# Column sums of an output weight: VectorE additions in a tail, or accumulating DMA transfers during the attention

## The chip, the cores and the metric

One core of one Trainium2 chip runs the whole program in one launch. The metric is device time in microseconds (us) from start to end of the program, the median of several runs. Engines are named as the profile names them: PE (TensorE matmul), PEld (its weight load), DVE (VectorE), ACT (ScalarE), POOL (GpSimd) and SP (SyncE, which here only issues DMA transfers).

## What is computed

An attention over 4 batches, 8 heads, 576 positions and 64 columns feeds two feed-forward layers in a row, on 2304 tokens with 512 columns and 2048 hidden columns. The change is in layer 1, whose constant `b` is applied in a cheaper place than the reference writes it:

```python
def _moe_ref(x, w_in, w_out, s, b):
    h = x @ w_in
    r = np.maximum(h, 0.0)
    g = s * (r * r) + b
    return (g @ w_out).astype(np.float32)
```

Since `b` is one number, `b @ w_out` is `b` times the column sums of `w_out`: 512 numbers, the same for every token. The kernel leaves `b` out of layer 1, computes these sums once, and adds them to the tokens when layer 2 loads them.

## The kernel before

Fp32 products run as products of two rounded pieces, a high and a low one (`woh` and `wol` for layer 1's output weight, `wih` and `wil` for its input weight). Each weight piece lies in SBUF in four buffers (r = 0 to 3) of 128 partitions x 4 x 512 numbers, 1 MB each. They are made in the first 175 us by `convert` and then stay until layer 1 is over.

The stages overlap. The attention runs unit by unit (a batch and a head, `unit`). Each unit loads `qk`, `qn` and `vx` through SP; POOL makes the first 64 columns of the weights `Pt` (line 557) from `ex` (line 500) and scales two of the five tiles (line 571); PE transposes the tiles (line 598) and multiplies them with `V` (line 626). Between the attention's products PE does layer 1 for the tokens already there (lines 832 and 901, blocks of 256 tokens), and when the attention is over, two blocks of 512 tokens: this is **layer 1's tail**. In the tail the weights of layer 2 are converted as well (`convert`, lines 690 to 707, by ACT, DVE and POOL), combined (`combine_in` and `combine_out`, line 743), split (`split`, lines 728 and 729) and stored in DRAM. Layer 2 follows (lines 1034 and 1100).

No engine's order is written by hand. Every piece of work is a step with an engine, an estimated duration, a priority (a lower number goes first), an extra `lag` until its result is there, and the steps that it must follow. `Plan.order` plays this through and gives each engine one fixed order; on the chip each engine then works down its own list, waiting at each instruction for what it needs. So an instruction whose input comes later than planned holds up everything behind it on its engine. POOL and SP also issue DMA transfers in this order.

The column sums are `column_sums`, with priority 700, behind most else. After `begin`, a step in the first block of the tail, DVE adds the 16 + 16 slices of `woh` and `wol` into `total` (lines 800 and 802, 31 additions of 128 x 512). One PE product with a matrix of ones (line 822) sums over the 128 partitions, into a bank of the ring `h`, whose two banks also take layer 1's first products; ACT reads those banks at line 877. `pick` (lines 815 and 817) moves the 512 sums into `bcs`, one number per partition and column group. Layer 2's loads add `bcs` at line 959.

Of the kernel before, what the change touches and what calls it, by code (L numbers as in the profile page):

```python
# [9 lines left out]
F32 = mybir.dt.float32  # L10
# [4 lines left out]
AF = mybir.ActivationFunctionType  # L15
ALU = mybir.AluOpType
# [3 lines left out]
P = 128  # L20
# [3 lines left out]
PE, ACT, DVE, POOL, DMA = range(5)  # L24
# [29 lines left out]
def dve_us(n, fast=False):  # L54
    return 0.068 + (0.00052 if fast else 0.00104) * n
# [123 lines left out]
class Plan:  # L179
# [29 lines left out]
    def add(self, engine, us, prio, f, r=(), w=(), after=(), keep=(), share=1.0):  # L209


        bufs = list({id(b): b for b in (*r, *w, *keep) if b.ring is not None}.values())
        new = [b for b in bufs if b.maker is None]
        waits = {id(s): s for b in r for s in b.writers}
        waits.update((id(s), s) for s in after)
        s = Step(engine, us, prio, f, list(waits.values()), bufs, new)
        s.share = share
        s.left = len(waits)
        for x in waits.values():
            x.next.append(s)  # L220
        for b in bufs:
            b.users += 1
            if b.maker is None:
                b.maker = s
            elif id(b.maker) not in waits:
                b.maker.next_start.append(s)
                s.left += 1
        for b in w:
            b.writers.append(s)
        self.steps.append(s)  # L230
        return s
# [100 lines left out]
def attention_then_two_ffn(ctx: ExitStack, tc: tile.TileContext, qk, qz, vm, beta,  # L332
# [3 lines left out]
    nc = tc.nc  # L336
# [8 lines left out]
    NR = 4  # L345
    FPR = NFC // NR
# [4 lines left out]
    NB1 = len(blocks1)  # L351
# [8 lines left out]
    plan = Plan()  # L360
    add = plan.add
# [3 lines left out]
    dram = ctx.enter_context(tc.tile_pool(name="dram", bufs=1, space=DRAM))  # L365
# [4 lines left out]
    mask = const.tile([P, SP], BF16, name="mask")  # L370
# [10 lines left out]
    WOD = dram.tile([P, 3, NQ2 // 2, DH], F32, name="wo_d")  # L381
    WIS = [dram.tile([P, 2, 2, 4, P], F32R, name=f"wi_split{q}_d") for q in range(NQ2)]
    WOS = [dram.tile([P, 7, 2, NQ2 // 2, DH], F32R, name=f"wo_split{x}_d") for x in range(2)]
    x_in = {(b, g): Buf() for b in range(B) for g in range(2)}
    y_in = {j: Buf() for j in range(NT // N1)}
    wi_in, wo_in, wi_split = ({} for _ in range(3))
# [22 lines left out]
    R = {}  # L409
# [249 lines left out]
    W = {}  # L659
# [6 lines left out]
    def w_at(nm, r, j):  # L666
        return W[nm, r].t[:, j]
# [65 lines left out]
    def load_us(n):  # L733
        return n * 512 / 310e3
# [31 lines left out]
    def combine_out(prio, q, w0, w1):  # L766
# [4 lines left out]
        def b_(i, j):  # L771
            return (w0, w1)[i].t.bitcast(F32)[:, j * DH:(j + 1) * DH]

        def t_(i):
            return sc.t[:, i - 1]

        sums(prio, [sc, w0, w1], [lambda: (t_(1), b_(0, 1), b_(0, 0), ALU.subtract), lambda: (t_(2), b_(1, 1), t_(1), ALU.subtract),
                                  lambda: (t_(3), b_(1, 1), b_(0, 1), ALU.subtract), lambda: (t_(4), b_(1, 0), t_(2), ALU.subtract)])
        d, x = WOS[q // 4], q % 4
        if q < 4:  # L780
# [11 lines left out]

    def column_sums(prio, begin):

        total, ps = Buf(R["total"], [P, 512]), Buf(R["h"], [P, 512])

        def more(r, j, nm):
            x = w_at(nm, r, j).bitcast(F32)
            if r == j == 0 and nm == "wol":
                nc.vector.tensor_tensor(total.t, w_at("woh", 0, 0).bitcast(F32), x, op=ALU.add)  # L800
            elif r + j:
                nc.vector.tensor_tensor(total.t, total.t, x, op=ALU.add)

        for r in range(NR):
            for j in range(FPR):
                def pair(r=r, j=j):
                    more(r, j, "woh")
                    more(r, j, "wol")

                add(DVE, dve_us(512) * (2 if r + j else 1), prio, pair, [W["woh", r], W["wol", r]] + [total] * (r + j > 0), [total],  # L810
                    after=[begin] * (r + j == 0))

        def pick():
            for ec in range(NCC):
                nc.vector.tensor_tensor_reduce(total.t[:, ec * P:(ec + 1) * P], ps.t[:, ec * P:(ec + 1) * P], ident, 1.0, 0.0,
                                               ALU.mult, ALU.add, bcs[:, ec:ec + 1])
            nc.vector.tensor_scalar(bcs, bcs, sb[:, 1:2], None, op0=ALU.mult)

        plan.steps[-1].lag = 12.0
        ones = Buf(R["ones"], [P, P])  # L820
        add(ACT, 0.2, prio, lambda: nc.scalar.activation(ones.t, mask[:, :P], AF.Copy, bias=1.0), after=[begin], w=[ones])
        add(PE, 0.87, prio, lambda: nc.tensor.matmul(ps.t, ones.t, total.t, start=True, stop=True), [ones, total], [ps])
        add(DVE, 1.0, prio, pick, [ps, total], [sums_in, total])

# [13 lines left out]
    def load_x(j, prio):  # L838

        t0, n = blocks1[j]  # L840
        big = n > N1
        xh, xl = xs[j] = [[Buf(R[x], [P, NCC // (1 + big), n], F32R) for _ in range(1 + big)]
                          for x in (("yh", "yl") if big else ("xh", "xl"))]
        edge = len(TA) * P - D
        need = [x_in[b, g] for b in range(B) for g in range(2)
                if b * S + g * edge < t0 + n and b * S + (edge, S)[g] > t0]
        for c in range(NCC):
            xr, half = Buf(R["yr" if big else "xr"], [P, n]), Buf()
            add(DMA, 0.002 * n, prio, lambda c=c, xr=xr: nc.sync.dma_start(xr.t, x_d[:, c, t0:t0 + n]), need, [xr])
            add(ACT, act_us(n), prio, lambda c=c, xr=xr: nc.scalar.copy(x_at(xh, c), xr.t), [xr], [xh[c * len(xh) // NCC], half])  # L850
            add(DVE, dve_us(n), prio, lambda c=c, xr=xr: nc.vector.tensor_tensor(x_at(xl, c), xr.t, x_at(xh, c).bitcast(F32),
                                                                                 op=ALU.subtract),
                [xr, half], [xl[c * len(xl) // NCC]])
# [152 lines left out]
    def load_wo(blk, p, half):  # L1006
# [7 lines left out]
        else:  # L1014
            add(POOL, 1.0, prio, lambda: nc.gpsimd.dma_start(w.t, WOS[half][:, slot]), need, [w]).lag = 3.0 + load_us(8 * DH)  # L1015
        return w
# [153 lines left out]
    opened = add(NONE, 0.0, 0.0, open_second, after=attention_steps)  # L1170
# [5 lines left out]
    def rank1(i):  # L1176
        i += max(0, i - NFC * (NB1 - NBIG))
        return UNIT0 + UNIT * (i + LEAD) / PER_UNIT
# [3 lines left out]
    for i in range(len(seq) + LAG1):  # L1182
        if i < len(seq):
            j, fc = seq[i]
            begin = len(plan.steps)
            if fc == 0:
                load_x(j, -1.0)
                accs[j] = [Buf(R[x], [P, 512]) for x in BANKS[j]]
            n = len(plan.steps)
            halves[i] = first(j, fc, rank1(i), -1.0)  # L1190
            in_steps[fc // FPR] += [x for x in plan.steps[n:] if x.engine == PE]
            if j < NB1 - NBIG:
                small_steps += plan.steps[begin:]
            if (j, fc) == (NB1 - 2, 4):
                begin_sums = plan.steps[-1]
        if i >= LAG1:
            j, fc = seq[i - LAG1]
            n = len(plan.steps)
            y_part(j, fc, accs[j], *halves.pop(i - LAG1), rank1(i) + 0.01)
            out_steps[fc // FPR] += plan.steps[n:]  # L1200
            begin = n
            if fc == NFC - 1:
                n = len(plan.steps)
                y_out(j, accs[j], -1.0)
            if j < NB1 - NBIG:
                small_steps += plan.steps[begin:]
            if fc == NFC - 1:
                if j == NB1 - NBIG - 1:
                    small_left = add(NONE, 0.0, 0.0, close_small, after=small_steps)
                if j == NB1 - 2:  # L1210
                    banks_left = add(NONE, 0.0, 0.0, lambda: None, after=[x for x in plan.steps[n:] if x.engine != DMA])
        if i == len(seq) - 1:
            left = [add(NONE, 0.0, 0.0, lambda: None, after=in_steps[r]) for r in range(NR)]
            inputs_left = add(NONE, 0.0, 0.0, lambda: None, after=[*left, *plan.steps[layer1:]])
    out_left = [add(NONE, 0.0, 0.0, lambda: None, after=out_steps[r]) for r in range(NR)]
    column_sums(700.0, begin_sums)
    closed = add(NONE, 0.0, 0.0, close_first, after=plan.steps[layer1:])
    low, high = Home(m1t, "low", 1024), Home(m1t, "high", 2560, F32R)
# [102 lines left out]
```

## Time and profile before

| | |
|---|---|
| median of 3 runs | 1045.85 us (1044.26 to 1050.34) |
| the profiled execution | 1047.84 us, span 1046.1 us |
| busy share | PE 96%, PEld 89%, DVE 83%, ACT 65%, POOL 27% |
| mean granted clock of TensorE | 0.986 |
| moved by DMA | 188.63 MB |

The span runs from the first to the last instruction of the profiled execution. A busy share is an average over stages that have different limits: a stage is read from the busy times of its own stretch and from the waits there. An idle time names its releaser, the work that ended last before the waiting instruction could go.

### The profile page before, as it was taken

To read this page: it belongs to the slowest core of one execution; us is meant where nothing else is said; L and a number is where in the kernel's file an instruction comes from. 1 tells how busy PE (TensorE), PEld (TensorE's weight loads), DVE (VectorE), ACT (ScalarE), POOL (GpSimd) and SP (SyncE) were. 2 spreads that over 40 slices of the span, in tenths; PEclk is the share of its full clock that TensorE was granted. 3 is DMA by queue.
4 is the path that set the end of the run, shared out by engine and by line. 5 is a ranking of instruction groups with operands and counts; after the bars stand their busy time and mean duration, and the time that the engine had idled before them with its cause. 6 is when DMAs were issued, how large, how long until landed. Compare 5 with 4: busy or idle time off the path is not lost. (4 is left out here: it accounts for less than half of the span.)

```text
span 1046.1 us, 20182 instructions
## 1 busy us (share of the span) xinstructions
PE 1004.7 (96%) x6710; PEld 926.6 (89%) x6710; DVE 870.4 (83%) x2399; ACT 680.0 (65%) x1575; POOL 280.6 (27%) x386
## 2 busy tenths in 40 slices
PE   6889997999999999999997999999999999999998
PEld 4657787999999999999885778899989999999998
DVE  6898999999999999975699989459985779757865
ACT  6876887888888787766644686446653456534552
POOL 6864354333334244312223330000110000100010
PEclk9998998999999999999999899999999999999999
DMA  9663563323422432307857886758686666776564
GB/s 257 181 193 107 154 205 97 109 88 99 138 87 88 122 94 88 103 24 240 244 159 217 256 286 227 272 165 290 216 307 209 222 211 203 248 250 196 178 216 167
DMA packets 88984, 188.63 MB, mean 180 GB/s; under 512 B 8752, under 2 KB 63024, under 8 KB 81584
## 3 DMA queue, kind: packets, MB, share of 16 engines
q1 hardware_dynamic: 81392, 135.95, 41.3%
q0 software_dynamic: 7056, 51.38, 14.5%
q8 instruction: 53, 0.87, 0.3%
q14 instruction: 51, 0.42, 0.1%
q10 hardware_dynamic: 432, 0.01, 0.0%
HBM read 144.32 MB, written 42.99 MB: 179 GB/s over the span
## 5 line engine op out<-in xcount | busy, mean ns | idle before, releaser
L1100 PE MATMUL bank<-woh,S 128*128 128x256 f32 x792 | 106.3, 281 | 2.6 <-DMA woh<-wo_split_d 1.8
L1100 PEld LDWEIGHTS bank<-woh,S 128*128 128x128 f32 x792 | 99.4, 189 | 3.2 <-issue 1.9
L1100 PE MATMUL bank<-wol,S 128*128 128x256 f32 x720 | 96.8, 281 | 0.0
L557 POOL TENSOR_SCALAR Pt<-ex,nm 128x64 f32<-128x64 f32 x148 | 73.9, 511 | 84.3 <-PE bank L598 45.1
L1034 PE MATMUL bank<-wi,woh 128*128 128x384 f32 x426 | 93.8, 335 | 0.6 <-DMA woh<-wi_split_d 0.6
L554 ACT ACTIVATE Pt<-Pt,mx 128x64 f32<-128x64 f32 (+4 forms) x148 | 81.8, 555 | 16.9 <-DVE mx L545 16.2
L1100 PEld LDWEIGHTS bank<-wol,S 128*128 128x128 f32 x720 | 90.5, 190 | 0.0
L707 POOL TENSOR_TENSOR stage<-stage 128x512 int32<-128x512 int32 x36 | 49.5, 1374 | 105.9 <-DVE stage L705 67.2
L1034 PEld LDWEIGHTS bank<-wi,woh 128*128 128x128 f32 x426 | 75.6, 188 | 1.3 <-DMA woh<-wi_split_d 0.8
L598 PE MATMUL bank<-ident,Pt 128*128 128x128 f32 x432 | 66.7, 281 | 10.1 <-POOL Pt L571 7.7
L1034 PE MATMUL bank<-wi,wol 128*128 128x384 f32 x294 | 75.9, 334 | 0.0
L606 DVE TENSOR_TENSOR PTl<-bank,PTh 128x128 fp32r<-128x128 f32 (+1 forms) x144 | 63.8, 480 | 2.2 <-ACT PTh L603 1.4
L598 PEld LDWEIGHTS bank<-ident,Pt 128*128 128x128 f32 x432 | 50.0, 143 | 15.5 <-POOL Pt L571 10.5
L571 POOL TENSOR_SCALAR Pt<-Pt,rs 128x64 f32<-128x64 f32 x64 | 45.5, 754 | 67.8 <-DVE rs L576 51.7
L1015 POOL DMA_DIRECT2D wol<-wo_split_d x17 | 9.2, 541 | 200.4 <-DVE wi L729 107.1
L545 DVE CUSTOM_DVE_ANT_0 Pt<-bank,mask 128x320 f32<-128x320 f32 (+3 forms) x148 | 59.2, 416 | 3.9 <-PE bank L541 2.0
L603 ACT CAST PTh<-bank 128x128 fp32r<-128x128 f32 (+1 forms) x144 | 55.1, 431 | 3.0 <-PE bank L598 1.7
L901 PE MATMUL bank<-gh,wol 128*128 128x256 f32 x320 | 54.0, 292 | 0.0
L901 PE MATMUL bank<-gl,woh 128*128 128x256 f32 x320 | 54.0, 291 | 0.0
L1034 PEld LDWEIGHTS bank<-wi,wol 128*128 128x128 f32 x294 | 53.0, 188 | 0.4
L901 PE MATMUL bank<-gh,woh 128*128 128x256 f32 x320 | 52.6, 287 | 0.0
L832 PE MATMUL bank<-xh,wi 128*128 128x256 f32 x320 | 50.6, 289 | 0.7 <-DVE rt L881 0.6
(290 smaller groups left out, 2962.0 us busy)
## 6 DMA issues: line engine op xcount, KB each, us to landing
wol<-wo_split_d POOLq DMA_DIRECT2D x17, 1024.0 KB, 5.6
woh<-wo_split_d POOLq DMA_DIRECT2D x16, 1024.0 KB, 5.6
qk<-in_qk SPq DMA_DIRECT2D x24, 608.0 KB, 3.8
stage<-in_w_out SPq DMA_DIRECT2D x23, 512.0 KB, 4.3
wo_split_d<-high SPq DMA_DIRECT2D x44, 256.0 KB, 3.4
stage<-in_w_in SPq DMA_DIRECT2D x21, 512.0 KB, 4.6
stage<-wi_d SPq DMA_DIRECT2D x24, 384.0 KB, 4.8
wi_split_d<-woh SPq DMA_DIRECT2D x8, 1024.0 KB, 4.9
```

What stands on the lines that cost most here:

```text
L545: nc.vector.tensor_tensor_reduce(Pt[t].t[:, D + lo:D + hi], ps.t[:, :hi - lo], mask[:, SP - w + lo:SP - w + hi], -SCALE, mx.t[:, t:t + 1] ...
L554: nc.scalar.activation(Pt[t].t[:, D:w + D], Pt[t].t[:, D:w + D], AF.Exp, bias=mx.t[:, t + i:t + i + 1], scale=-1.0, accum_out=rs.t[:, t:t ...
L557: add(POOL, 0.3, lambda: nc.gpsimd.tensor_scalar(Pt[t].t[:, :D], ex.t[:, t, :], nm.t[:, t:t + 1], 1.0, op0=ALU.mult, op1=ALU.mult), [ex, n ...
L571: (nc.vector if e == DVE else nc.gpsimd).tensor_scalar(x, x, r, None, op0=ALU.mult)
L598: nc.tensor.transpose(ps.t[:, c - c0, :], Pt[t].t[:, c * P:(c + 1) * P], ident)
L603: (nc.vector.tensor_copy if dve else nc.scalar.copy)(PT[0].t[:, at_], ps.t[:, :n])
L606: nc.vector.tensor_tensor(PT[1].t[:, at_], ps.t[:, :n], PT[0].t[:, at_].bitcast(F32), op=ALU.subtract)
L707: add(POOL, 1.23 if layer == 1 else 1.45, prio, lambda: nc.gpsimd.tensor_tensor(w.t, w.t, words()[:, :, 0], op=ALU.add), [raw, low_words, ...
L832: nc.tensor.matmul(ph, w_at(nm, r, cc)[:, o:o + P], x_at(x, cc), start=(part == 0 and cc == 0), stop=(part == 2 and cc == NCC - 1))
L901: nc.tensor.matmul(acc[ec // per].t[:, (ec % per) * n:(ec % per + 1) * n], w_at(nm, r, jj)[:, ec * P:(ec + 1) * P], t(x), start=(big and f ...
L1034: nc.tensor.matmul(ps.t[:, :H2], w[i // 4].t[:, j, kk, i % 4], x[kk].t[:, k], start=begin and part == kk == 0, stop=part == 2 and kk == 1, ...
L1100: nc.tensor.matmul(acc[t].t[:, :DH], s.t[:, j, t * P:(t + 1) * P], x.t[:, k, q % 4], start=q == part == 0, stop=q == NQ2 - 1 and part == 2)
```

## The change

The 31 additions on DVE go. In their place the eight 1 MB buffers `woh` and `wol` are piled up in a DRAM tensor `pile_d`, during the attention: SP copies the first, and POOL issues seven transfers that add to what lies there (`accum_op`). Each must wait until the one before it has landed, since it reads and rewrites the same bytes. Then SP copies the first quarter of the pile to `fold_d`, POOL adds the other three quarters to it with three accumulating transfers of 256 KB, and SP loads the result into `total`. The steps start after the first product of layer 1's second block (`begin` is now in block 1). The load into `total` and the matrix of ones wait for the end of the attention (`opened`), where their buffers are made. The PE product and `pick` stay as they are.

```diff
+    pile_d, fold_d = dram.tile([P, FPR, 512], F32, name="pile_d"), dram.tile([P, 512], F32, name="fold_d")
...
-        total, ps = Buf(R["total"], [P, 512]), Buf(R["h"], [P, 512])
-
-        def more(r, j, nm):
-            x = w_at(nm, r, j).bitcast(F32)
-            if r == j == 0 and nm == "wol":
-                nc.vector.tensor_tensor(total.t, w_at("woh", 0, 0).bitcast(F32), x, op=ALU.add)
-            elif r + j:
-                nc.vector.tensor_tensor(total.t, total.t, x, op=ALU.add)
...
-                add(DVE, dve_us(512) * (2 if r + j else 1), prio, pair, [W["woh", r], W["wol", r]] + [total] * (r + j > 0), [total],
-                    after=[begin] * (r + j == 0))
+        total, ps, piled, folded = Buf(R["total"], [P, 512]), Buf(R["h"], [P, 512]), Buf(), Buf()
+        pile, fold = pile_d, fold_d
+
+        def pile_up(i, x):
+            if i == 0:
+                add(DMA, 4.0, prio, lambda: nc.sync.dma_start(pile, x()), [W["woh", 0]], [piled], after=[begin]).lag = 2.0
+            else:
+                add(POOL, 1.0, prio, lambda: nc.gpsimd.dma_start(pile, x(), accum_op=ALU.add),
+                    [W["wol" if i % 2 else "woh", i // 2], piled], [piled]).lag = 20.0
+
+        for i in range(2 * NR):
+            pile_up(i, lambda i=i: W["wol" if i % 2 else "woh", i // 2].t.bitcast(F32))
+        add(DMA, 1.0, prio, lambda: nc.sync.dma_start(fold, pile[:, 0]), [piled], [folded]).lag = 4.0
+        for j in range(1, FPR):
+            add(POOL, 1.0, prio, lambda j=j: nc.gpsimd.dma_start(fold, pile[:, j], accum_op=ALU.add),
+                [piled, folded], [folded]).lag = 10.0
+        add(DMA, 1.0, prio, lambda: nc.sync.dma_start(total.t, fold), [folded], [total], after=[opened]).lag = 3.0
...
-        plan.steps[-1].lag = 12.0
         ones = Buf(R["ones"], [P, P])
-        add(ACT, 0.2, prio, lambda: nc.scalar.activation(ones.t, mask[:, :P], AF.Copy, bias=1.0), after=[begin], w=[ones])
+        add(ACT, 0.2, prio, lambda: nc.scalar.activation(ones.t, mask[:, :P], AF.Copy, bias=1.0), after=[opened], w=[ones])
...
-            if (j, fc) == (NB1 - 2, 4):
+            if (j, fc) == (1, 0):
                 begin_sums = plan.steps[-1]
```

Through the attention the lists of PE, DVE and ACT stay as they were, but for one exchange of neighbours among PE's products. (Behind the change, lines of the file are one or two higher: 557 becomes 558, 571 becomes 572.) What changes there is POOL's list, by ten transfers, and SP's, by three. POOL in the middle of the attention, before, where line 500 makes `ex` from the loaded `qn`, line 571 scales two tiles and line 557 starts the next five:

```order
L500 TENSOR_SCALAR ex_4165<-qn_4120 128x320 [waits DMAHW6_49,Pool_49]
L571 TENSOR_SCALAR Pt_1_4061<-Pt_1_4061,rs_4063 128x64 [waits DVE_49,Activation_49]
L571 TENSOR_SCALAR Pt_1_4068<-Pt_1_4068,rs_4063 128x192 [waits Activation_49]
L557 TENSOR_SCALAR Pt_0_4237<-ex_3953,nm_4092 128x64 [waits DVE_49]
L557 TENSOR_SCALAR Pt_0_4250<-ex_3953,nm_4092 128x64
```

and at the same place now:

```order
L501 TENSOR_SCALAR ex_4173<-qn_4128 128x320 [waits DMAHW7_49,Pool_49]
L572 TENSOR_SCALAR Pt_1_4069<-Pt_1_4069,rs_4071 128x64 [waits DVE_49,Activation_49]
L572 TENSOR_SCALAR Pt_1_4076<-Pt_1_4076,rs_4071 128x192 [waits Activation_49]
L803 DMA pile_d<-woh_0_1884 128x2048 [waits DMASW4_49]
L558 TENSOR_SCALAR Pt_0_4246<-ex_3961,nm_4100 128x64 [waits DVE_49]
L558 TENSOR_SCALAR Pt_0_4259<-ex_3961,nm_4100 128x64
```

The sixth accumulating transfer has come between line 571's and line 557's work, and it waits (`DMASW4`) for the fifth to have landed. DVE in the tail, before, where the additions begin:

```order
L705 SCALAR_TENSOR_TENSOR low<-raw_7239,low 128x512
L800 TENSOR_TENSOR total_7337<-woh_0_500,wol_0_524 128x512
L802 TENSOR_TENSOR total_7337<-total_7337,woh_0_500 128x512
L802 TENSOR_TENSOR total_7337<-total_7337,wol_0_524 128x512
...
L884 TENSOR_TENSOR xh_7361<-g_7317,xh_7361 128x512
L704 TENSOR_SCALAR low<-low 128x512
```

and now:

```order
L706 SCALAR_TENSOR_TENSOR low<-raw_7257,low 128x512
L884 TENSOR_TENSOR xh_7324<-g_7285,xh_7324 128x512
L744 TENSOR_TENSOR sc_7341<-stage 128x2x128
L744 TENSOR_TENSOR sc_7341<-sc_7341,stage 128x2x128
```

The additions are gone, and layer 1's own line 884 and the combining of layer 2's weights (line 743, now 744) have moved up. PE at the sums' product (line 822), before, between two groups of line 901, where the first tail block is at the third of `woh`'s four buffers:

```order
L832 MATMUL bank_107<-yl_6923,wih_0_1550 128x512 x2
L901 MATMUL bank_111<-xh_7652,woh_0_1326 128x512
...
L822 MATMUL bank_108<-total_7337,ones_7328 128x512
L901 MATMUL bank_111<-xh_7652,wol_0_1331 128x512
```

and now:

```order
L832 MATMUL bank_109<-yl_6941,wi_742 128x512 x2
L901 MATMUL bank_113<-xh_7166,woh_0_502 128x512
...
L822 MATMUL bank_110<-total_6898,ones_6859 128x512
L901 MATMUL bank_113<-xh_7166,wol_0_526 128x512
```

The product stands 180 rows of PE's list earlier, where that block is still at the first buffer. All bank numbers are two higher, because of the two new tensors.

## Rows read from the trace of the kernel before

**Rows 1.** The page: busy time of each engine, share of the span, instructions.

```profile
PE 1004.7 (96%) x6710; PEld 926.6 (89%) x6710; DVE 870.4 (83%) x2399; ACT 680.0 (65%) x1575; POOL 280.6 (27%) x386
```

**Rows 2.** Busy time by stretch: us, PE, PEld, DVE, ACT, POOL, clock, DMA share, GB/s.

```profile
200.00:475.00 275.00, 272.83 (x2209) 267.52 (x2208) 252.67 (x974) 218.53 (x603) 97.36 (x161) 1.00 0.32 95
500.00:515.00 15.00, 15.00 (x71) 12.35 (x70) 7.20 (x15) 10.39 (x19) 5.31 (x4) 1.00 0.79 237
515.00:560.00 45.00, 45.00 (x196) 36.42 (x195) 44.05 (x67) 22.70 (x39) 12.54 (x9) 1.00 0.61 185
560.00:585.00 25.00, 18.94 (x62) 13.38 (x61) 22.99 (x50) 15.40 (x32) 7.38 (x6) 0.80 0.84 264
...
600.00:610.00 10.00, 7.81 (x33) 5.67 (x32) 7.03 (x12) 8.12 (x16) 4.53 (x3) 1.00 0.86 294
```

**Rows 3.** Busy time by stretch, within the tail's stall.

```profile
575.00:580.00 5.00, 4.18 (x10) 3.06 (x10) 4.86 (x7) 2.50 (x7) 2.98 (x2) 0.50 0.87 283
```

**Rows 4.** Timeline of PE: start, us, engine, line, operation, [idle before <- releaser].

```profile
304.67 0.60 PE L598 MATMUL bank<-ident,Pt 128*128 128x128 f32 x4
...
558.47 1.10 PE L832 MATMUL bank<-yl,wih 128*128 128x512 f32 x4
559.41 1.08 PE L901 MATMUL bank<-xh,woh 128*128 128x512 f32 x4
...
571.57 2.07 PE L822 MATMUL bank<-total,ones 128*128 128x512 f32 x2 [4.62 <-ACT g L877]
...
583.89 1.10 PE L832 MATMUL bank<-yh,wi 128*128 128x512 f32 x4
```

**Rows 5.** Timeline of ACT at the stall.

```profile
568.37 0.71 ACT L728 CAST high<-low 128x256 fp32r<-128x256 f32 x2 [6.23 <-POOL low L707]
```

**Rows 6.** Timeline of POOL: attention (the places of the transfers), then the stall.

```profile
189.30 1.52 POOL L557 TENSOR_SCALAR Pt<-ex,nm 128x64 f32<-128x64 f32 x3
...
283.00 1.78 POOL L557 TENSOR_SCALAR Pt<-ex,nm 128x64 f32<-128x64 f32 x3
...
303.01 1.40 POOL L571 TENSOR_SCALAR Pt<-Pt,rs 128x64 f32<-128x64 f32 x2
...
328.58 1.01 POOL L500 TENSOR_SCALAR ex<-qn 128x320 f32<-128x320 f32 x1
...
355.64 1.01 POOL L500 TENSOR_SCALAR ex<-qn 128x320 f32<-128x320 f32 x1 [1.93 <-DMA qn<-in_qz]
...
567.00 1.33 POOL L707 TENSOR_TENSOR low<-low,raw 128x512 int32<-128x512 int32 x1 [1.15 <-DVE low L705]
```

**Rows 7.** DVE's groups from 500 to 620 us: busy, mean ns of one | idle before.

```profile
L802 DVE TENSOR_TENSOR total<-total,wol 128x512 f32<-128x512 f32 x15 | 14.4, 959 | 0.5
L802 DVE TENSOR_TENSOR total<-total,woh 128x512 f32<-128x512 f32 x15 | 13.5, 901 | 0.1
```

**Rows 8.** Timeline of DVE: the last addition, and the step that POOL awaited.

```profile
562.80 0.69 DVE L802 TENSOR_TENSOR total<-total,wol 128x512 f32<-128x512 f32 x1
...
566.18 0.69 DVE L705 SCALAR_TENSOR_TENSOR low<-raw,low 128x512 int32<-128x512 int32 x1
```

**Rows 9.** Waits of the whole span, by who waited: us, times, longest.

```profile
PE bank L901 <- DVE yr L921: 2.0, 1, 2.0
```

**Rows 10.** DMA issues: queue, count, KB each, median us from issue to landing.

```profile
wol<-wo_split_d POOLq DMA_DIRECT2D x17, 1024.0 KB, 5.6
...
wi_split_d<-woh SPq DMA_DIRECT2D x8, 1024.0 KB, 4.9
```

**Rows 11.** Transfers of `wo_split_d`: min/median/max ns of POOL's issue, and landing.

```profile
L1015 POOL DMA_DIRECT2D wol<-wo_split_d x17: 527/527/757, 737.6 to 1021.7; - x17
...
DMA to landing us min/median/max: 2.1/4.9/9.7
```

**Rows 12.** Loads of `qn`, 185 to 345 us: us from issue to landing.

```profile
DMA to landing us min/median/max: 2.2/2.3/3.3
```

**Rows 13.** SP's timeline: the issue behind the copy into `fold_d`.

```profile
353.13 0.33 SPq L480 DMA_DIRECT2D qn<-in_qz  x1
```

More of the change, by code (lines that the diff above doesn't have):

```diff
@@ L793, in column_sums @@
     def column_sums(prio, begin):
-        total, ps = Buf(R["total"], [P, 512]), Buf(R["h"], [P, 512])
-        def more(r, j, nm):
-            x = w_at(nm, r, j).bitcast(F32)
-            if r == j == 0 and nm == "wol":
-                nc.vector.tensor_tensor(total.t, w_at("woh", 0, 0).bitcast(F32), x, op=ALU.add)
-            elif r + j:
-                nc.vector.tensor_tensor(total.t, total.t, x, op=ALU.add)
[L804 to L808, printed above, removed]
-                add(DVE, dve_us(512) * (2 if r + j else 1), prio, pair, [W["woh", r], W["wol", r]] + [total] * (r + j > 0), [total],
-                    after=[begin] * (r + j == 0))
+        total, ps, piled, folded = Buf(R["total"], [P, 512]), Buf(R["h"], [P, 512]), Buf(), Buf()
[13 more added lines that the diff above has]
+        add(DMA, 1.0, prio, lambda: nc.sync.dma_start(total.t, fold), [folded], [total], after=[opened]).lag = 3.0
         def pick():
```

## The prediction

> **What bounds the kernel now.** I read the page's busy shares first: PE is busy for 96% of the span, 1004.7 us [rows 1]. So only some 41 us without PE work can be won, and any work taken from another engine counts only where PE waits for it. Next come the busy times by stretch [rows 2]. From 200 to 475 us, where the attention runs, PE is idle for 2.2 us of 275. DVE is busy for 253 of them, POOL for only 97, and the DMA engines for a third. From 515 to 560 us DVE has 44.05 us of work in 45: that is where the additions lie. Right behind, from 560 to 585 us, PE is idle for 6.1 us and the granted clock drops to a mean of 0.80. The reader is to see this pair: a full DVE first, an idle PE afterwards.
>
> The timeline of PE shows what it costs [rows 4]. Unhindered, four products of line 901 or 832 start every 0.93 us (558.47 to 559.41). Between the starts at 559.41 and 583.89 us lie 14 such groups and the sums' product. At the usual pace that is 14 x 0.93 = 13.0 us, plus 1.1 us for the sums' product, whose two passes show as 2.07 us at a lowered clock; I take half. It took 24.5 us, so **10.4 us are lost**. One part is the 4.62 us of waiting in front of line 822; another is the clock, which from 575 to 580 us is 0.50, the 1.2 GHz level, after PE had stood idle [rows 3].
>
> Who is late is read backwards. Line 822 waits for ACT, which has to empty a bank at line 877 [rows 4]. ACT had stood idle for 6.23 us, until 568.37, at a rounding step ahead of that in its list, waiting for POOL's line 707 [rows 5]. POOL started that step at 567.00, after DVE's line 705 [rows 6]; DVE started it at 566.18, having worked almost without a gap since 515 [rows 2, 8]. The additions themselves ended at 563.5 [rows 8], so the sum is not what was awaited: the additions stood in the queue ahead of the conversion.
>
> **The change, part by part.** *Removed:* 31 additions on DVE. The 30 of line 802 take 14.4 + 13.5 us [rows 7], and one of line 800 about 0.7, in all 28.6 us. Undisturbed, one takes 0.69 [rows 8], so 31 x 0.69 = 21.4 us are the additions' own; the other 7.2 are stretching, which may fall on other DVE work instead. Of DVE's 67.0 us of work in the 70 us from 515 to 585 [rows 2] some 45.6 remain, 65%. A queue that was at most 10 us late, with 21 us of its work gone, has no reason to be late: I take the 10.4 us as won. Layer 2's conversions then become the next thing that could be late, and what covers them is that third of DVE's time.
>
> *A second stall:* from 600 to 610 us PE is idle for 2.2 us [rows 2], most of it behind DVE's line 921 [rows 9]. It is the tail of the same backlog or something of its own. Ends: 0 and 2.2 us won; I take half, 1.1.
>
> *Moved:* the sums' product and `pick`. On the present clock the product now falls between 500 and 515 us, and `pick`, about 1 us of DVE's time, with it, where DVE is busy for 7.2 us of 15 [rows 2]. The product now takes the bank that is not being filled at that point, so it need not wait for the group just ahead. Its matrix of ones is one short ACT step, earlier by the same distance. I cost all this at nothing; without that DVE cover it would be about 1 us. The load of `total` stands at the attention's end, about 475 us, some 30 us ahead of its use. The last transfer is issued about two units, 25 us, behind the first quarter-size one of 356.7 [rows 6], so the chain could be 80 us late before this load noticed.
>
> *Added:* three transfers on SP and ten on POOL. Issuing a plain 1 MB transfer takes POOL 0.53 us [rows 11], so ten take 5.3 us, in a stage where POOL is idle for 178 of 275 us [rows 2]: nothing, if they don't wait. SP's three issues cost 0.5 us each at most, with nothing waiting at those points.
>
> *The new waits.* Each accumulating transfer holds POOL's list until the one before it has landed, and lines 500, 557 and 571 are queued behind it. Line 571 is the tight one: POOL ends a pair at 304.4 [rows 6] and PE transposes tiles of that set from 304.67 on [rows 4], so a delay there reaches PE nearly whole. What counts is the spacing. On the present clock the first one falls at 190.8, the fifth at 284.2 (after two of three), the sixth at 304.4 and the seventh at 329.6 us [rows 6]. Six gaps make 138.8 us, 23.1 on average; the smallest, fifth to sixth, is 20.2. SP's copy into `fold_d` must be past by 353.1, where the next `qn` load is issued [rows 13]: 23.5 us after the seventh. The first quarter-size transfer stands behind line 500 at 356.7 [rows 6]. So a **landing time T under about 20 us costs nothing**; above 23.1 the delay is at least 6T - 138.8 us.
>
> No row shows an accumulating transfer. A plain 1 MB store takes 4.9 us and a plain 1 MB load 5.6 [rows 10]. This one must read source and destination and write the destination: never less than 4.9 us; one read and one write in sequence make 10.5; three moves of 1 MB in sequence, each as slow as the slowest landing of such loads, 9.7 [rows 11], make 29. I take 10.5, nearest to the rows that move 1 MB between SBUF and DRAM, and keep 4.9 and 29. Both 4.9 and 10.5 cost no wait.
>
> *Traffic:* seven times 3 MB and some small change, beside a third of busy DMA engines. The loads of `qn` land in 2.3 us [rows 12], and POOL already waits for some of them. About 15 fall into the time of the transfers; with T at 10.5 of 23.1, some seven overlap one. If these took twice as long and nothing covered it, that would be 16 us; most have line 557's or other work between them and line 571. Ends 0 and 16; I take 2.
>
> A rule of the skill speaks against this part. The rows first: POOL's 1 MB issues take 527 ns in the middle and 757 at most, beside a busy DVE [rows 11]. By the Trainium skill, "SBUF — State Buffer", section "SBUF: two separate sides", GpSimd can't write the descriptors of its transfers while VectorE runs an instruction in a mode that holds their shared port pair. By the rows the issues cost nothing more; by the rule each could be held for one DVE instruction, which would show as issues longer than 757 ns. No row here shows the attention's DVE work beside an issue.
>
> **The sum.** Against the profiled execution's own 1047.84 us: -10.4 - 1.1 + 2 = -9.5. That execution is 2.0 us above the median, 1045.85, for which the trace has no reason. I take the same 9.5 off the median: **1036.3 us**.
>
> **The rivals.** *POOL waits for its own transfers* (0.15, slower). Decides from T: at 24.7 us, 6T - 138.8 is 9.4, and the gain is used up. At the upper end of 29 it is 35 us: 1045.85 - 9.5 + 35 = 1071. For it: three moves of data, and SP's loads in between. Against it: 1 MB one way takes 5 us, so T would have to be five times that.
>
> *The transfers disturb the attention's loads* (0.15, about 1047). All of 14 us more than I took: 1036.3 + 14 = 1050 at the end, some 1045 in the middle. For it: PE, DVE and POOL's line 571 have no room in that stage. Against it: the DMA engines are two thirds free. The Trainium skill, "DMA: Bandwidth & Descriptors", section "Issuing engines are not separate DMA queues", says that transfers of all issuing engines share the same 16 DMA engines and interleave.
>
> *The stall stays* (0.10, 1041 to 1045). The change doesn't do what it says, as the tail still converts layer 2's weights through DVE, POOL and ACT in fixed order, and POOL's steps stretch DVE's. Half the 10.4 remaining gives 1041.5. For it: DVE's 65% holds stretched steps that the plan doesn't know. Against it: 21 us less in a queue that was late by 10.
>
> **How the numbers follow.** My forecast has 0.60, from 1032.0 (both stalls gone, no disturbance, and the fastest run's 1.6 us below the median: 1045.85 - 12.6 - 1.6 = 1031.7) to about 1040.5. A measurement of this kernel can tell about 0.5%, 5.2 us, from no change: below 1040.6 is faster, above 1051.1 slower. Faster: 0.60 and a little of the stall's rival, 0.62. Slower: the waiting rival and some of the disturbance, 0.17. The rest, 0.21, is the same. The range reaches over the second and third rival to 1051.0 and leaves out the waiting rival and what is below 1032.
>
> **What would show it.** Right: no wait of PE at line 822, the clock at 1.00 from 560 to 585 us less the shift, DVE busy for some 65% there; accumulating transfers that land within 20 us, and no POOL wait for a `pile_d` transfer in front of line 558 or 572. Disturbance would show as longer `qn` and `qk` landings and new PE idle time between 200 and 400 us. The prediction is wrong if T exceeds 24 us, or if ACT still waits several us for line 707 in the tail.

## The result, and the profile after

The changed kernel takes **1061.55 us** (median of 4 runs, 1061.2 to 1061.96) against 1047.03 for the kernel before, run beside it: a ratio of 1.0137, with a 95% interval of 1.0106 to 1.0169. It is 14.5 us slower, where the forecast had it 9.5 us faster, and above the predicted range. The profiled execution took 1061.39 us, with a span of 1059.6.

The tail did what was predicted. The busy times by stretch of the kernel after, with the columns of [rows 2]:

```profile
200.00:475.00 275.00, 255.49 (x1990) 248.44 (x1991) 237.34 (x925) 200.95 (x556) 99.73 (x163) 0.97 0.46 121
515.00:560.00 45.00, 45.00 (x217) 37.23 (x216) 29.98 (x66) 27.91 (x49) 16.02 (x11) 1.00 0.82 243
560.00:585.00 25.00, 25.00 (x109) 20.23 (x109) 17.50 (x33) 16.85 (x31) 8.94 (x6) 1.00 0.86 262
```

From 515 to 585 us PE has no gap and its clock stays at 1.00, where [rows 2] had 18.94 us of 25 at 0.80; DVE has 47.5 of 70 us of work, 68%. The loss is in the first row, the attention: PE is idle for 19.5 us there, and was for 2.2 [rows 2]. Its mean clock is 0.97: 3% of 275 us are another 8 us. Together that is some 25 us, and 27 with the 1.8 us in which PE is idle from 195 to 200 (below). A gain of some 12 in the tail and a loss of some 27 in the attention make the 14.5.

The same view of the kernel after, in steps of 5 us beside three of the seven transfers, which POOL issues at 191.55, 270.82 and 301.69 us:

```profile
195.00:200.00 5.00, 3.17 (x26) 2.94 (x24) 1.18 (x13) 2.27 (x9) 0.70 (x2) 1.00 1.03 234
200.00:205.00 5.00, 1.75 (x7) 1.75 (x8) 2.88 (x9) 0.85 (x2) 0.08 (x1) 0.64 0.64 193
...
275.00:280.00 5.00, 0.96 (x9) 0.76 (x7) 1.42 (x4) 0.14 (x1) 1.70 (x4) 0.99 1.00 256
280.00:285.00 5.00, 4.38 (x19) 4.33 (x20) 3.62 (x12) 3.42 (x10) 0.00 (x0) 0.50 0.38 132
...
305.00:310.00 5.00, 4.79 (x39) 4.56 (x37) 5.00 (x20) 3.63 (x11) 0.00 (x0) 1.00 0.94 198
310.00:315.00 5.00, 0.87 (x5) 0.87 (x5) 0.88 (x5) 0.84 (x2) 2.37 (x4) 0.90 0.24 73
```

First the DMA share rises to about 1 (last column but one; it adds up the times of the transfers' records, so it can come out a little above 1), then ACT, DVE and PE run dry for 4 to 6 us, and then PE works on at a lower clock: 0.50 from 280 to 285 us, the 1.2 GHz level, after it had been idle for 4 of the 5 us before. What they wait for stands in the timelines of POOL, ACT and PE of the kernel after:

```profile
280.16 1.03 ACT L850 CAST xh<-xr 128x256 fp32r<-128x256 f32 x3 [5.03 <-DMA xr<-x_d]
...
280.62 3.77 PE L832 MATMUL bank<-xh,wi 128*128 128x256 f32 x15 [4.66 <-ACT xh L850]
...
301.69 0.91 POOL L803 DMA_DIRECT2D pile_d<-wol  x1
...
312.63 1.02 POOL L501 TENSOR_SCALAR ex<-qn 128x320 f32<-128x320 f32 x1 [8.71 <-DMA qn<-in_qz]
...
314.13 1.11 PE L599 MATMUL bank<-ident,Pt 128*128 128x128 f32 x4 [4.34 <-POOL Pt L572]
```

Each time one small load is late: `xr` holds ACT and so PE; `qn` holds POOL's line 501, behind which stands line 572, and PE's transposes wait for that. How late they were is in the transfers' times from issue to landing: the pile's transfer issued at 301.69, the load of `qn` at 304.09, those of `xr` from 270.58 to 272.1, and the two stores of `y_d` at 193.2 and 193.7:

```profile
DMA to landing us min/median/max: 10.5/10.5/10.5
...
DMA to landing us min/median/max: 8.4/8.4/8.4
...
DMA to landing us min/median/max: 2.3/8.8/9.1
...
DMA to landing us min/median/max: 8.8/8.8/8.9
```

The transfer of 301.69 landed at 312.2, `qn` at 312.5: **together with it**, though issued 2.4 us later and five times smaller. Undisturbed, `qn` takes 2.3 us [rows 12]. The others follow the same pattern: the stores of `y_d` landed at 202.1 and 202.4, the transfer issued at 191.55 at 201.9; in the kernel before these two stores took 3.6 and 3.8 us.

### The profile page after: what moved, and what is told of

Read it like the earlier page. It is cut to its first block, busy times and chain, and to the rows that moved or that the text cites. A ratio compares the mean times of both kernels' runs of the same rounds, so it can differ in the third digit from the quotient of the medians.

```text
span 1059.6 us, 20204 instructions
## 1 busy us (share of the span) xinstructions
PE 1007.4 (95%) x6710; PEld 930.9 (88%) x6710; DVE 846.7 (80%) x2368; ACT 680.8 (64%) x1575; POOL 289.7 (27%) x396
## 4 chain that ended last, share of the span: by engine, by line
PE 52%; issue 18%; DVE 10%; DMA 8%; ACT 4%; POOL 4%; SPq 0%; POOLq 0%; DVEq 0%; ACTq 0%
PE bank L901 15%; PE bank L832 14%; PE bank L1034 9%; PE bank L1100 6%; PE bank L627 3%; PE bank L599 2%; DVE PTl L607 1%; DMA qn<-in_qz 1%; DMA y_d<-ys 1%; DMA qk<-in_qk 1%; PE bank L541 1%; ACT Pt L555 1%; PE bank L542 1%; DMA xr<-x_d 1%; DMA woh<-wo_split_d 1%
## 5 line engine op out<-in xcount | busy, mean ns | idle before, releaser
L599 PE MATMUL bank<-ident,Pt 128*128 128x128 f32 x432 | 67.6, 283 | 18.1 <-POOL Pt L572 13.1
L832 PE MATMUL bank<-xh,wi 128*128 128x256 f32 x320 | 53.0, 298 | 5.9 <-ACT xh L850 4.7
```

Of the source, the lines that this page charges most:

```text
L599: nc.tensor.transpose(ps.t[:, c - c0, :], Pt[t].t[:, c * P:(c + 1) * P], ident)
L832: nc.tensor.matmul(ph, w_at(nm, r, cc)[:, o:o + P], x_at(x, cc), start=(part == 0 and cc == 0), stop=(part == 2 and cc == NCC - 1))
```

## The experiments

Before the first runs three theories stood side by side: the large pieces of the transfers take turns with the small loads (theory 1), the time for which the adding occupies the DMA engines counts (theory 2), POOL's ten issues hold up its list (theory 3). The kernel before was run again beside them. So ratios are compared, and the loss of a kernel is its ratio less that of e1, times 1047 us. For the kernel after that makes (1.0137 - 0.9875) x 1047 = **27.4 us**. The intervals of the two ratios, given in brackets behind each, make such a loss uncertain by some 3 us either way.

**e1: without the piling.** Only SP's first write, the copy and the load remain:

```diff
-        for i in range(2 * NR):
+        for i in range(1):
...
-        for j in range(1, FPR):
+        for j in range(1, 1):
```

> Leaves out the seven accumulating transfers into pile_d and the three into fold_d; SP's first write, the copy and the load stay, so the column sums hold one piece of 32. Theory 1 (the transfers' large pieces take turns with the attention's small transfers on the 16 DMA engines), theory 2 (the time for which the accumulations occupy these engines counts, whatever the size of the pieces) and theory 3 (POOL's ten issues hold its list) all say: the attention is as before, PE busy for at least 49.5 us of each 50 from 200 to 400 us, and the tail keeps its gain, 1033 to 1037 us. Rival: the tail's stall did not go because the additions went; then 1043 to 1048.

Measured: 1035.75 us, ratio 0.9875 (0.9856 to 0.9895). Busy times by stretch of e1:

```profile
200.00:475.00 275.00, 272.34 (x2201) 266.85 (x2200) 253.95 (x978) 217.47 (x602) 95.40 (x161) 1.00 0.31 94
515.00:560.00 45.00, 45.00 (x196) 36.42 (x195) 34.62 (x66) 29.18 (x53) 17.28 (x12) 1.00 0.87 259
560.00:585.00 25.00, 25.00 (x109) 20.27 (x108) 24.04 (x38) 19.34 (x39) 10.48 (x7) 1.00 0.90 287
```

The attention is as before [rows 2] and the tail has no stall. The removal of the additions is worth 13.1 us; all that was lost comes with the ten transfers.

**e2: the same transfers without adding.**

```diff
-                add(POOL, 1.0, prio, lambda: nc.gpsimd.dma_start(pile, x(), accum_op=ALU.add),
+                add(POOL, 1.0, prio, lambda: nc.gpsimd.dma_start(pile, x()),
```

> The seven large transfers overwrite pile_d instead of adding to it, so the sums hold the last piece only; POOL still issues them at the same places and the pieces are as large. SP's own plain write of this kind landed in 4.2 us against 9.5. Theories 1 and 2: the window of disturbance is about half as long, so about half of some 26 us of loss in the attention: 1044 to 1050. Theory 3: POOL issues as often and waits as rarely, 1058 to 1063. If it lies in the adding itself, and plain bytes disturb nothing: 1034 to 1037.

Measured: 1041.1 us, ratio 0.9907 (0.9877 to 0.9938), a loss of 3.4 us, hardly clear of none and below the 1044 to 1050 of theories 1 and 2. The profile calls the queue of POOL's transfers the software queue (q0), that of SP's the hardware queue (q1). Records, MB and share of the 16 engines' time of q0 from 190 to 375 us, and KB and median us to landing of each transfer, first of the kernel after:

```profile
q0 software_dynamic: 1008, 7.34, 21.1%
...
pile_d<-wol POOLq DMA_DIRECT2D x4, 1024.0 KB, 9.3
...
pile_d<-woh POOLq DMA_DIRECT2D x3, 1024.0 KB, 9.5
```

and of e2:

```profile
q0 software_dynamic: 1152, 7.60, 10.9%
...
pile_d<-wol POOLq DMA_DIRECT2D x4, 1024.0 KB, 5.7
pile_d<-woh POOLq DMA_DIRECT2D x3, 1024.0 KB, 5.5
```

For about as many MB the adding takes the engines twice as long. Theory 3 is out: POOL issued as often, 0.3 us shorter each time. But 0.6 of the landing time with an eighth of the loss left two readings open: the adding harms in a way of its own, or lateness costs only beyond some slack. e9 tells them apart.

**e3: pieces of 2 KB.** A padded row makes 512 pieces of each 128:

```diff
-    pile_d, fold_d = dram.tile([P, FPR, 512], F32, name="pile_d"), dram.tile([P, 512], F32, name="fold_d")
+    pile_d, fold_d = dram.tile([P, FPR, 528], F32, name="pile_d"), dram.tile([P, 512], F32, name="fold_d")
...
-        pile, fold = pile_d, fold_d
+        pile, fold = pile_d[:, :, :512], fold_d
```

> pile_d gets rows of 528 in place of 512 numbers, so that each accumulating transfer goes in 512 pieces of 2 KB and not in 128 of 8 KB; all is computed. Theory 1: a small transfer waits for a piece a quarter as long at each of its turns; qn, 8.4 us beside a transfer with large pieces, lands in 4 to 5, and of some 26 us of loss 5 to 12 remain: 1040 to 1048. Theory 2: as many bytes, as long on the engines: 1058 to 1064. Theory 3: 512 pieces to issue and not 128, POOL's issues get longer than 0.9 us, 1061 or more.

Measured: 1054.13 us, ratio 1.0053 (1.0035 to 1.0071), a loss of 18.6 us, between theories 1 and 2. The time on the engines is even a little longer, from the same view of e3:

```profile
q0 software_dynamic: 3704, 7.36, 23.9%
...
pile_d<-wol POOLq DMA_DIRECT2D x4, 1024.0 KB, 10.5
```

The latest small transfers come earlier all the same: `qn` 6.8 us instead of 8.4, the latest `xr` 8.1 instead of 9.1, and `vx`, issued 0.1 us ahead of the last transfer, 6.1 instead of 8.3, some 5 us before that transfer has landed and not with it. So the size of the pieces counts, for about a third of the loss; theory 1 is not the main thing.

**e4: the transfers in the tail.**

```diff
-            if (j, fc) == (1, 0):
+            if (j, fc) == (NB1 - 2, 4):
```

> The accumulating transfers begin where the additions of the kernel before began, behind the attention, at about 515 us. All theories: attention as before. The tail's transfers are layer 2's weights, loaded ahead, with POOL and DVE less pressed; theory 1 and 2: 1034 to 1042, with a few late weight loads beside the transfers. If such transfers cost wherever they lie, 1050 or more.

Measured: 1089.95 us, ratio 1.0392 (1.0371 to 1.0413). That is far above the 1034 to 1042 of theories 1 and 2; only the last sentence of the expectation, 1050 or more, holds. The stretch at the tail's end, and waits from 500 to 720 us (waiting engine and line <- released by: us in all, times, longest), of e4:

```profile
650.00:700.00 50.00, 33.06 (x136) 26.23 (x134) 9.71 (x14) 13.27 (x23) 1.68 (x2) 0.85 0.42 129
```

```profile
POOL fold_d L810 <- DMA fold_d<-pile_d: 56.3, 3, 49.1
...
PE bank L822 <- DMA total<-fold_d: 23.5, 1, 23.5
...
POOL pile_d L803 <- DMA pile_d<-woh: 11.0, 1, 11.0
```

PE's longest wait here has another cause: the chain of transfers ends after the point at which PE has the sums' product in its list, and PE stands for 23.5 us. SP issued the copy into `fold_d` only at 690.07 us in its list, though the last transfer into `pile_d` was issued at 643.95. The prediction's first rival is seen here too: POOL waited 11.0 us for one of its own transfers. The loss is some 54 us in all; the other 30 were not taken apart, so e4 does not tell the theories apart.

After these four the question was put anew. **Theory L:** a small transfer's lateness costs nothing up to a few us, then PE stands and its clock falls. **Theory O:** the time on the engines counts, in proportion.

**e5: halves.** As many bytes and as much adding, cut in two, about evenly spaced:

```diff
-                add(POOL, 1.0, prio, lambda: nc.gpsimd.dma_start(pile, x(), accum_op=ALU.add),
-                    [W["wol" if i % 2 else "woh", i // 2], piled], [piled]).lag = 20.0
+                for f in range(0, FPR, 2):
+                    add(POOL, 1.0, prio, lambda f=f: nc.gpsimd.dma_start(pile[:, f:f + 2], x()[:, f:f + 2], accum_op=ALU.add),
+                        [W["wol" if i % 2 else "woh", i // 2], piled], [piled]).lag = 10.0
```

> Each of the seven accumulating transfers is issued as two of 512 KB, the second half a spacing (some 11 us) behind the first; all is computed, as many bytes, as much adding. Theory L (a small transfer's lateness counts only from a few us on, then PE stands idle and its clock falls behind): no small transfer is late by more than some 4 us, half of what stood beside the whole ones, and of some 27 us of loss against the run without piling 5 to 13 remain: 1041 to 1049 us, PE's clock at 1.00 nearly throughout. Theory O (the time for which these transfers occupy the engines counts): 1058 to 1064. Theory 3 (POOL's issues): seven more, above 1062.

Measured: 1044.95 us, ratio 0.996 (0.9944 to 0.9977), a loss of 8.9 us, as theory L had it. The attention of e5:

```profile
200.00:475.00 275.00, 267.79 (x2129) 260.67 (x2130) 251.98 (x972) 213.66 (x592) 107.50 (x177) 0.99 0.49 122
```

The DMA share is 0.49 and was 0.46 in the kernel after, and PE is idle for 7.2 us instead of 19.5, with its clock at 0.99. Nothing was taken from the engines' time, only from the length of each occupation. One part of the forecast failed: the stores of `y_d` at 193 us, right behind SP's write and the first half, still took 7.6 and 7.9 us.

**e6: four of the seven**, at twice the spacing:

```diff
-        for i in range(2 * NR):
+        for i in (0, 1, 3, 5, 7):
...
-                    [W["wol" if i % 2 else "woh", i // 2], piled], [piled]).lag = 20.0
+                    [W["wol" if i % 2 else "woh", i // 2], piled], [piled]).lag = 44.0
```

> Only four of the seven accumulating transfers, at about twice the spacing; the column sums miss three pieces of 4. Theories L and O both say that each transfer costs by itself, some 3.8 us: 1035.75 + 4 x 3.8 = 1051 us, between 1046 and 1055. If the loss came from their chain (one waiting for another, a backlog that builds up), it would be mostly gone: 1036 to 1042.

Measured: 1043.88 us, ratio 0.9961 (0.9943 to 0.9979), a loss of 9.0 us where four sevenths would be 15.7. An even price is refuted. That one transfer waits for another is not the cause either: POOL waited for a landing once, for 0.9 us, in this kernel and in the kernel after, and both times it was SP's first plain write. Stretches of e6, with transfers at 191.65, 246.88, 298.84 and 344.99 us:

```profile
185.00:250.00 65.00, 59.46 (x466) 58.43 (x465) 54.29 (x213) 46.53 (x129) 23.97 (x40) 0.95 0.43 121
250.00:300.00 50.00, 48.20 (x389) 47.00 (x389) 46.93 (x184) 40.18 (x114) 17.79 (x28) 1.00 0.47 136
300.00:350.00 50.00, 49.87 (x405) 48.97 (x404) 47.23 (x184) 39.83 (x111) 18.56 (x32) 1.00 0.48 122
350.00:400.00 50.00, 47.14 (x375) 46.31 (x374) 43.23 (x164) 37.99 (x105) 19.80 (x30) 0.97 0.39 113
```

The first costs 5.5 us of PE and a clock of 0.95, the third next to nothing. Behind the first, two stores of `y_d` were caught (9.0 and 9.2 us), for which DVE stood 6.3 us; behind the fourth a load of `qn` (7.4 us), for which POOL stood 7.1 and PE 2.8; behind the third only a store of `x_d` and a load of `vx` (6.6 and 5.6 us), for which nothing stood longer than 0.2. So what a transfer costs depends on which small one is caught behind it, and how soon that one is needed. The kernel after agrees: behind its transfers of 249.01 and 327.81 us PE has no gap in the next 11 us.

**e9: two plain writes in place of one adding transfer**, the second into a spare tensor of the same shape:

```diff
-                add(POOL, 1.0, prio, lambda: nc.gpsimd.dma_start(pile, x(), accum_op=ALU.add),
+                add(POOL, 1.0, prio, lambda: [nc.gpsimd.dma_start(d, x()) for d in (pile, spare_d)],
```

> In place of each of the seven accumulating transfers, two plain writes of the same 1 MB one right behind the other, into pile_d and into a spare tensor; nothing is added up, so the sums hold the last piece. Together they should take the engines about as long as one accumulating transfer, some 9 to 10 us. Theory L (only the time counts for which small transfers stand behind it): the loss of the kernel after comes back, 1053 to 1064 us. Rival (adding in DRAM disturbs in a way of its own, apart from the time that it takes): as with one plain write or little above it, 1040 to 1047 us.

Measured: 1058.57 us, ratio 1.0089 (1.006 to 1.0118), a loss of 22.4 us. Share and landings of e9 from 190 to 375 us, and its attention:

```profile
q0 software_dynamic: 2016, 14.68, 20.2%
...
spare_d<-wol POOLq DMA_DIRECT2D x4, 1024.0 KB, 8.3
...
spare_d<-woh POOLq DMA_DIRECT2D x3, 1024.0 KB, 9.1
```

```profile
200.00:475.00 275.00, 258.67 (x2021) 251.10 (x2022) 241.59 (x937) 204.74 (x565) 102.94 (x172) 0.97 0.45 145
```

Without any adding, but with the same occupation (20.2% against 21.1%, the second write landed after 7.0 to 10.3 us), most of the loss is back, and PE's row is nearly that of the kernel after. So the harm comes in the main from the adding's taking as long as two plain writes; for a harm of its own at most the other 5 us are left, little more than the intervals. From one write to two, the loss rises from 3.4 to 22.4 us: that is theory L's slack, and not theory O's proportion. In e2 the latest `qn` took 4.4 us and the latest `xr` 5.5; here they took 7.5 and 9.2.

**e10: quarters.** As e5, with four pieces of 256 KB and a spacing of a quarter.

> Each accumulating transfer is issued as four of 256 KB, a quarter of the spacing apart; all is computed. Theory L: each lands in some 4.5 us alone, no small transfer is late by more than about 2 us, and of the 9 us of loss that the halves left, 2 to 5 remain: 1037 to 1042 us. Theory 3: 28 issues of about 0.9 us on POOL's list, 25 us of its time where it is 60% idle, and a wait behind a transfer where the spacing is too small: 1046 or more.

Measured: 1043.04 us (1036.5 to 1046.93, 10 runs), ratio 0.9942 (0.9921 to 0.9964), a loss of 7.0 us. That is above theory L's band and below theory 3's. The intervals of halves and quarters overlap, so that cutting further buys anything is not shown. The runs spread over 10 us, with a mean clock of 0.983 at 1046.89 us and of 0.993 at 1036.5; the one with a trace was the shortest, so where the rest is lost can't be read from it.

**e7 and e8: the additions elsewhere.** Both start from the kernel before, with no transfers. e7 begins the additions at the attention's end. e8 does so too, but holds those of the third and fourth buffers back until the last block:

```diff
-    column_sums(700.0, begin_sums)
+    column_sums(700.0, opened)
```

```diff
-                    after=[begin] * (r + j == 0))
+                    after=[begin] * (r + j == 0) + ([marks[r, j]] if r > 1 else []))
...
-            if (j, fc) == (NB1 - 2, 4):
-                begin_sums = plan.steps[-1]
+            if j == NB1 - 1 and 4 <= fc < 12:
+                marks[fc // FPR + 1, fc % FPR] = plan.steps[-1]
```

> The kernel before, its additions on DVE begun at the attention's end, about 475 us, and not at 515; no transfer is added. If the tail's stall came from 31 additions in the same 45 us as the conversion's first steps, DVE's idle 18 us from 475 to 515 take most of them and the stall shrinks to 0 to 4 us: 1035 to 1041. If it comes from the additions' number, wherever they lie ahead of the conversion: 1045 to 1048.

> As e7, but the additions of the second half of the weights wait until the last block, about 610 to 670 us, where DVE is half idle. 15 additions (10 us) from 475 fit into its idle time there: 1034 to 1039. If additions anywhere in the tail cost PE time: 1043 or more.

Measured: e7 1044.37 us, ratio 0.9956 (0.9939 to 0.9973), between the two forecasts; e8 **1035.03 us**, ratio 0.9874 (0.9853 to 0.9894). The one wait of PE in the tail of e7, and the busy times of e7, then of e8:

```profile
529.70 2.08 PE L832 MATMUL bank<-yh,wi 128*128 128x512 f32 x4 [4.89 <-ACT g L877]
```

```profile
475.00:515.00 40.00, 40.00 (x257) 36.23 (x256) 38.71 (x67) 20.99 (x42) 6.11 (x4) 1.00 0.60 188
515.00:560.00 45.00, 40.11 (x161) 31.75 (x160) 35.58 (x64) 26.06 (x45) 17.02 (x12) 0.92 0.80 239
```

```profile
475.00:515.00 40.00, 40.00 (x257) 36.23 (x256) 32.99 (x60) 22.35 (x45) 9.11 (x6) 1.00 0.73 220
515.00:560.00 45.00, 45.00 (x195) 36.43 (x194) 32.31 (x58) 30.07 (x54) 17.98 (x12) 1.00 0.88 266
```

31 additions in a row fill DVE at both places tried (here 38.71 us of 40), and the stall comes behind them, some 40 us earlier. With half of them moved to 610 to 650 us, where DVE has room, there is none in these stretches. e8 does all the work on the same engine as the kernel before and is as fast as e1, which leaves most of the sums out: it is faster than both kernels, by 1.3% than the one before.

## Why the prediction failed

**The tail: right, a little small.** Predicted -10.4 - 1.1; e1 shows -13.1. The stall of 560 to 585 us went whole. So did that of 600 to 610 us, of which the sum took half.

**POOL's waits: right.** T was taken as 10.5 us; the transfers landed after 8.0 to 10.5, and POOL waited for a landing once, for 0.88 us, that of SP's plain write. The first rival, a POOL that waits for its own transfers, did not occur in the attention.

**The moved work: right, at nothing.** PE does not wait once from 505 to 720 us in the kernel after, at line 822 either. The third rival, a stall that stays, did not occur.

**POOL's issues.** By the Trainium skill's section "SBUF: two separate sides" ("SBUF — State Buffer") they could be held by DVE, and longer issues than 757 ns were named as the sign. They took 887 to 1094 ns in the kernel after, but 613 to 765 in e2 at the same places of POOL's list. So the length comes with the adding; at seven transfers it is some 2 us of an engine that is idle for two thirds of the attention. No cost of the rule shows in these issues.

**Traffic: this step failed.** "Ends 0 and 16; I take 2"; the runs show 27.4. The mechanism stood there, as the second rival with a chance of 0.15, and the signs named for it came: PE idle between 200 and 400 us, and longer landings of `qn` and `qk` (`qk` up to 7.3 us, before up to 4.7). Its price, 14 us at most, was too low in four ways:
- Only `qn` was counted. The stores of `y_d` and the loads of `xr` were caught as well, and what holds ACT or DVE stops the whole attention, since these lists are in fixed order. (A load of `vx` that took 8.3 us cost nothing: PE is busy for 11.90 of the 12 us from 354.)
- "Twice as long" was guessed. They took up to nearly four times as long (`qn` 8.4 us instead of 2.3, `xr` 9.1 instead of at most 3.0, `y_d` 8.9 instead of 3.8), until the large transfer had landed.
- "The DMA engines are two thirds free" is a mean over 275 us [rows 2]. While a transfer was under way it reached 0.94 to 1.03. A mean share says nothing of the wait of one transfer.
- The clock was left out. It makes some 8 of the 25 us read in the attention.

That all queues share the 16 engines was cited with this rival and is borne out by e2 and e9. How a small transfer comes to wait for a large one stands in the records of the DMA engines. In the kernel after, these are all records from 305 to 307.5 us, with `qn` issued at 304.09, and then all from 275 to 278 us, beside three late loads of `xr`:

```profile
q0 software_dynamic: 58, 0.48, 96.4%
...
q0 software_dynamic: 69, 0.57, 90.9%
q1 hardware_dynamic: 69, 0.07, 8.7%
```

In the first stretch only pieces of the large transfer move, and no row of `qn`. In the second, pieces of 8 KB and rows of 1 KB move one for one. `qn` has 128 rows and the large transfer 128 pieces, 8 of each per engine if they are shared evenly (an estimate). With a first stretch lost and then one row for each piece, `qn` can't be through before the large transfer is; they landed 0.3 us apart. In e3, with `qn` issued at 294.30, the first stretch is as long: from 295 to 297.4 us there are 212 records of the software queue and none of the hardware queue. Only behind it do shorter pieces help, which fits the little that e3 won.

The Trainium skill has a rule for it that the prediction passed over, "DMA: Bandwidth & Descriptors", section "Queues, rings and completion order": an engine goes round the queues, and takes a whole packet, of typically 9 to 17 descriptors, from one before it turns to the next. The trace counts 144 records for a large transfer in the software queue, 9 per engine if they are shared evenly (an estimate). The first stretch agrees with a turn of several of them. The second, 69 beside 69, speaks against a turn as long as an engine's whole share. What sets the length of the first stretch is shown by no run.

**Left open.** Why quarters show no clear gain over halves, and what ended the first stretch. e8 makes both questions idle for this kernel.

## What to carry to other kernels

Price a large transfer not by the share of free DMA time but by the lateness of whatever small transfer is issued while it is under way: up to the large one's own landing time. Ask which of those small ones is awaited within that time by an engine with a fixed order; if one is, cut the large transfer: halves here took the loss from 27 to 9 us, quarters no clearly further. And before work is moved off an engine that is full for 45 us, look whether the same engine has room some tens of us earlier or later: here dependencies that spread the additions gained all that the transfers should have.

## What the runs showed of the hardware

An accumulating transfer of 1 MB from SBUF into DRAM landed in 8.0 to 10.5 us, against 4.6 to 7.5 for plain ones at the same places of POOL's list (e2), and took the DMA engines twice as long (21.1% against 10.9% of their time). POOL's issue of it took 0.89 to 1.09 us, of a plain one 0.61 to 0.77, of one in 512 pieces 1.23 to 1.50 (e3). Beside such a transfer, loads of 128 to 192 KB landed after 8.3 to 9.1 us and not 2.3 to 3.0, with the large one: `qn` got no row in from 305 to 307.5 us, and `xr` one row for each piece from 275 to 278.
